# Attention and two MLP layers on one core: layer two takes its query tiles in pairs, with new PSUM shares and a new order

## The chip, the cores and the metric

One core of a Trainium2 chip runs the whole program. Its engines run side by side, each through its own list of instructions in order: TensorE (PE; its weight loads are shown as PEld), VectorE (DVE), ScalarE (ACT), GpSimd (POOL), and SyncE (SP), which here issues every DMA. They wait for each other by semaphores. The metric is the device time of one execution in microseconds (us); lower is better.

## The reference

Attention over 4 batches of 8 heads (576 queries and keys, head size 64), in which each query keeps its 32 largest scores; then two layers over the 2304 rows of 512 numbers. All in float32.

```python
scores = scale * np.matmul(q, k.transpose(0, 1, 3, 2))
kth = np.partition(scores, -top_k, axis=-1)[..., -top_k:-top_k + 1]
scores = np.where(scores >= kth, scores, -1000000000.0)
attn = np.exp(scores - np.max(scores, axis=-1, keepdims=True))
attn = attn / (np.sum(attn, axis=-1, keepdims=True) + 1e-09)
x = np.matmul(attn, v)                     # rows of 8 heads x 64 side by side
h = x @ w_in                               # layer 1: 512 -> 2048
x = np.maximum(0.01 * h, h) @ w_out        #          2048 -> 512
r = np.maximum(x @ w_in2, 0.0)             # layer 2
out = (s * (r * r) + b) @ w_out2
```

## The kernel before

**Precision.** Every float32 operand of a product is split into two float16 halves, a high and a low one, and a product is made of three: high by high, high by low, low by high. For that the rows and weights are first scaled by powers of two (`pow2_steps`).

**Query tiles and units.** The rows are 18 tiles of 128 queries; two of them are split and take 64 queries of each of two batches. A tile has four units of two heads, 72 in all. For a unit TensorE makes the scores (`qk`, L842; a split tile needs twice the products), ScalarE copies them out of PSUM (`s_ev`, L848), VectorE finds the 32 largest by four rounds of MAX8 (`t_max`, L860) and three of match-and-replace (`t_rep`, L869) per head, then exponentials and the mask follow either by way of VectorE (`expo`, `mask`, L882 and L885) or of POOL and ScalarE (`above`, `less`, `expo2`, L895 to L901); a letter of `MKE` and `MK` chooses for each unit. The result is cast to two halves (`e_hi` L970, `e_lo` L976) and turned by DMA (`e_turn`, L980); the first `EB` units are turned on TensorE instead (`e_tr2`, `e_sub`). TensorE multiplies by the values (`pv_mm`, L1010), VectorE brings the result out of PSUM (`x_ev`, L1017).

**Weights.** All four matrices are converted on the chip, each in 16 units of 128 columns or rows, four of them to a group with one scale: layer two's first (`2o`, `2i`), whose halves go back to DRAM (`sc16`), then layer one's (`1i`, `1o`), which stay in SBUF (`wreg`). A unit is loaded (`w_load`), rounded (`w_rest`, `w_shift`, `w_sign`, `w_round`), its group's norm is made on TensorE (`w_norm` L412, `sc_sum` L439), and it is split by one of five ways that a letter of `WM` names: `G` scales on VectorE (`pre`, L496) and `A` on ScalarE (L494), both with a subtraction on POOL (`lo_g`, L499); `D` uses ScalarE and VectorE (`lo_d`, L502); `P` and `V` multiply by a scaled identity on TensorE in float32 (`lo_t`, L507) into the ring `h`, copy the high half (`hi_p`, L513), and take the low half by another product and copy (`lo_s` L510, `lo_e` L516) or on VectorE (`lo_v`, L519). When all groups of layer one have their scales, `finals1` (the last line is L594) makes the constants without which no layer can start its activation.

**Layers.** `layer` makes one layer for one block of query tiles. `rows_in` scales, splits and turns the rows (a DMA, L1081). `m_in` (L1135) is 12 products that multiply one unit of the first weight, as stationary operand of 128 columns, by the block's turned rows; 512 columns fill a bank of the ring `h`. ScalarE and POOL make the two halves of the activation (`a1`, `a3`, `a4`, `a5`; L1164 to L1183). `m_out` (L1205) is 3 products for one unit of the second weight and one tile, 512 columns each, into the tile's bank `acc`. Layer one reads its weights from `wreg`. Layer two streams them from DRAM, two units (512 KB) a load (L1114), through four buffers (`wst`); one load of each weight is kept. `BLOCKS` has 16 blocks of one tile and one of two, for both layers; so layer two reads its weights 17 times.

**PSUM.** Eight banks: `tp` 2 (turned pieces, norms, sums, value products), `sc` 1 of two banks' size, `acc` 2, `h` 2.

**What sets the order.** The order of the instructions is not the engines' choice. `Plan` holds every step with an engine, an assumed duration, its dependences, the ring buffers it takes and a key. `order` plays the program once before it is built: whenever an engine is free it takes the ready step with the lowest key. The result is a fixed list per engine. The keys count in units of attention: `W0` and `WD` place the weights' conversion, `KO` the loads of keys, values and queries, and a layer's key `base` lies above all attention, so that layers fill TensorE between attention steps.

```python
        ready = {e: [] for e in set(self.eng)}
...
                heapq.heappush(ready[self.eng[n]], (self.key[n], n))
...
        base = 2.0 * sum(len(b) for b in blocks[:i]) + (1.0 if l else 0.0)
```

## Time and profile before

| | |
|---|---|
| median of 3 runs | 1210.54 us (1208.18 to 1210.85) |
| profiled execution, span | 1206.6 us |
| TensorE busy | 1044.3 us |
| VectorE, ScalarE, POOL busy | 918.5, 892.5, 844.5 us |
| DMA moved | 251.15 MB |

The page gives no other time for the profiled execution than its span, 3.9 us below the median of the runs. Idle time in one engine means little by itself; it matters on the engine that sets the end in that stretch. Records of products overlap in the trace, so the spacing of their starts is the price of a product, not the length of its record.

### The profile page before, as it was taken

The numbers are of one execution on the slowest core, as the hardware profiler recorded it, in microseconds if no ns is written. First come the engines' busy times: TensorE is split into PE (matmuls) and PEld (weight loads), VectorE is DVE, ScalarE is ACT, GpSimd is POOL, SyncE is SP. The second block draws the span as 40 slices with busy tenths as digits, with TensorE's granted clock in tenths as the row PEclk, the third lists the DMA queues.
The fourth block names the chain that finished last, engine by engine and source line by source line (L and its number), as shares of the span: only waits on it lengthen the run. The fifth ranks groups of instructions, "written<-read, shape, count | busy, mean of one in ns | idle before, by whom it ended". The sixth has DMA issues, their size and how long they took to land.

```text
span 1206.6 us, 30307 instructions
## 1 busy us (share of the span) xinstructions
PE 1044.3 (87%) x11589; PEld 754.8 (63%) x11589; DVE 918.5 (76%) x2164; ACT 892.5 (74%) x1696; POOL 844.5 (70%) x1169
## 2 busy tenths in 40 slices
PE   1675666239999999999999989999999999999988
...
GB/s 273 272 255 235 267 218 53 91 99 162 118 258 215 272 204 229 227 188 256 232 267 265 203 215 207 232 210 259 183 252 218 206 233 191 256 215 128 91 225 146
DMA packets 378289, 251.15 MB, mean 208 GB/s; under 512 B 281632, under 2 KB 306208, under 8 KB 378144
## 3 DMA queue, kind: packets, MB, share of 16 engines
...
q8 instruction: 90, 1.47, 0.5%
q14 instruction: 55, 0.45, 0.1%
...
## 4 chain that ended last, share of the span: by engine, by line
PE 43%; DVE 17%; DMA 12%; ACT 11%; POOL 11%; issue 4%; SPq 2%; DVEq 0%; POOLq 0%; ACTq 0%
PE h L1135 17%; PE acc L1205 17%; DVE mx L860 7%; DVE wk L869 6%; DMA st_o<-sc_2o 4%; PE pv L1010 3%; PE sc L842 3%; POOL ehl L976 2%; DMA a<-ehl 2%; POOL g L1183 2%; DMA st_i<-sc_2i 2%; POOL em L898 2%; ACT wreg L386 1%; ACT wreg L397 1%; ACT em L901 1%
## 5 line engine op out<-in xcount | busy, mean ns | idle before, releaser
L860 DVE MAX8 mx<-wk 128x8 f32<-128x576 f32 x432 | 313.2, 747 | 0.9
L1135 PEld LDWEIGHTS <-wreg 128*128 128x128 f16 x3264 | 211.0, 99 | 54.0 <-issue 6.4
L1135 PE MATMUL h<-early,wreg 128*128 128x128 f16 (+1 forms) x3264 | 235.1, 224 | 2.8 <-ACT r L1164 2.8
L1205 PE MATMUL acc<-wreg,g 128*128 128x512 f16 x864 | 231.3, 379 | 0.0
L1205 PEld LDWEIGHTS <-g 128*128 128x128 f16 x1728 | 154.8, 98 | 122.2 <-issue 17.3
L869 DVE MATCH_REPLACE8 wk<-mx,wk 128x576 f32<-128x576 f32 x288 | 212.8, 741 | 0.0
L1205 PE MATMUL acc<-st_o,g 128*128 128x512 f16 x756 | 200.6, 382 | 12.5 <-DMA st_o<-sc_2o 11.8
L1135 PEld LDWEIGHTS <-st_i 128*128 128x128 f16 x2856 | 179.7, 98 | 48.9 <-DMA st_i<-sc_2i 12.5
L1135 PE MATMUL h<-xT,st_i 128*128 128x128 f16 (+1 forms) x2856 | 201.4, 223 | 9.1 <-DMA st_i<-sc_2i 9.0
L976 POOL TENSOR_TENSOR ehl<-em,ehh 128x576 f16<-128x576 f32 x132 | 169.2, 1289 | 19.5 <-DMA a<-ehl 7.0
L898 POOL TENSOR_TENSOR em<-s,em 128x576 f32<-128x576 f32 x110 | 155.9, 1432 | 22.9 <-ACT em L895 22.7
L1183 POOL TENSOR_TENSOR g<-early,g 128x512 f16<-128x512 f32 x72 | 83.7, 1164 | 79.5 <-ACT g L1180 73.8
L842 PE MATMUL sc<-kT,qT 128*128 128x288 f16 (+1 forms) x640 | 102.3, 301 | 42.3 <-ACT s L848 36.4
L860 DVE MAX8 mx<-s 128x8 f32<-128x576 f32 x144 | 107.9, 750 | 23.0 <-ACT s L848 22.7
L1183 POOL TENSOR_TENSOR g<-r,g 128x512 f16<-128x512 f32 x72 | 84.4, 1172 | 49.7 <-ACT g L1180 49.3
L895 ACT ACTIVATE em<-s,st 128x576 f32<-128x576 f32 x110 | 82.2, 768 | 41.9 <-POOL st L889 37.5
L848 ACT COPY s<-sc 128x576 f32<-128x576 f32 x144 | 91.0, 632 | 23.5 <-PE sc L842 23.1
L901 ACT ACTIVATE em<-em,st,est 128x576 f32<-128x576 f32 x110 | 94.7, 862 | 17.1 <-POOL em L898 16.8
L869 DVE MATCH_REPLACE8 wk<-mx,s 128x576 f32<-128x576 f32 x144 | 106.8, 742 | 0.0
L1180 ACT ACTIVATE g<-r 128x512 f16<-128x512 f32 x144 | 89.5, 622 | 18.5 <-PE acc L1205 17.8
L842 PEld LDWEIGHTS <-qT 128*128 128x128 f16 (+1 forms) x640 | 56.9, 105 | 70.7 <-issue 49.9
L1167 ACT ACTIVATE r<-h,cg 128x512 f32<-128x512 f32 x72 | 49.1, 682 | 67.0 <-PE h L1135 65.9
...
## 6 DMA issues: line engine op xcount, KB each, us to landing
st_i<-sc_2i SPq DMA_DIRECT2D x119, 512.0 KB, 4.9
st_o<-sc_2o SPq DMA_DIRECT2D x119, 512.0 KB, 5.1
wreg<-in_moe_w_in_dram SPq DMA_DIRECT2D x32, 512.0 KB, 5.2
wreg<-in_moe_w_out_dram SPq DMA_DIRECT2D x16, 512.0 KB, 5.0
raw_1o<-in_moe_w_out_dram SPq DMA_DIRECT2D x16, 512.0 KB, 4.2
...
```

The lines of the kernel that those rows point to most:

```text
L842: nc.tensor.matmul(pt[a, c, 0:288], lhsT=qT[u][:, h, z, a], rhs=kT[b, p][:, 576 * h + 288 * c:576 * h + 288 * c + 288], start=(z == 0), st ...
L848: nc.scalar.copy(sc[u, h], box["pt"][:, :, 0:288])
L860: nc.vector.max(out=mx[u][:, h, r, :], in_=wk[u, h] if r else flat(sc[u, h]))
L869: nc.vector.match_replace(out=wk[u, h], in_to_replace=mx[u][:, h, r, :], in_values=src, imm_value=NEG)
L895: nc.scalar.activation(em[u][:, h, :], flat(sc[u, h]), AF.Relu, bias=st[u][:, 8 + h:9 + h], scale=-BIG)
L898: nc.gpsimd.tensor_tensor(em[u][:, h, :], flat(sc[u, h]), em[u][:, h, :], op=ALU.subtract)
L901: nc.scalar.activation(em[u][:, h, :], em[u][:, h, :], AF.Exp, bias=st[u][:, h:h + 1], scale=est[:, 0, u:u + 1], accum_out=st[u][:, 2 + h: ...
L976: nc.gpsimd.tensor_tensor(ehl[u][1][:, a], em[u][:, h, :], ehl[u][0][:, a], op=ALU.subtract)
L1135: nc.tensor.matmul(box["h"][:, n * T:(n + 1) * T], lhsT=w[:, ew, c, :], rhs=src[:, ex, c, :], start=(c == 0 and ew == 0 and ex == 0), stop ...
L1180: nc.scalar.activation(gt[:, 0], box["r1"], AF.Square if l else AF.Copy)
L1183: nc.gpsimd.tensor_tensor(ghl[i, l, g][:, 1], box["v"], ghl[i, l, g][:, 0], op=ALU.subtract)
L1205: nc.tensor.matmul(accs[i, l, tt], lhsT=ghl[i, l, g][:, eg, n * T + tt * P:n * T + (tt + 1) * P], rhs=w[:, ew], start=(f == 0 and eg == 0 ...
```

## The change

Five things change together.

- `BLOCKS` becomes nine pairs and holds for layer two alone; layer one takes each tile by itself. Layer two's `m_in` has 256 columns (two weight units fill a bank of `h`), and one loaded weight serves two tiles. The two tiles' rows for layer two (`xT1`) are one buffer; each tile's rows for layer one (`xT0`) get their own, four of half the size.
- PSUM: `tp` goes from two banks to one, `acc` from two to three. The norms (`w_norm`) and the column sums (`csum`) move from `tp` to `acc`.
- The letters: `WM` sends all 16 units of `1i` through TensorE (`P`), `2o` by `V` and `P`, `2i` by `P` and `A`, `1o` by `A` and `D`; `MK` and `MKE` have four masks fewer on VectorE; `EB` is 4 instead of 6.
- The finishing instructions `f1`, `f3`, `f4` use one-tensor forms with a scalar per row.
- The order: all keys are new, and ten tables add an offset to each step's key (of a unit's attention, of a weight's rounding, halves and load, of keys, values, queries, layers and rows). Some assumed durations are new too.

```diff
-        "ahh": 1, "ahl": 1, "x32": 1, "xs": 2, "xhl": 3, "xT0": 2, "xT1": 2, "r1": 2, "r2": 2, "g": 3, "raw": 2, "T": 8, "hl": 8, "wraw": 4, "wT": 8, "wst": 4,
-        "tp": 2, "sc": 1, "acc": 2, "h": 2, "lane": 1, "fin": 4, "nred": 1, "cI": 1}
-WM = {"1i": "PDAA", "1o": "DAAG", "2o": "GPPV", "2i": "PPAV"}
+        "ahh": 1, "ahl": 1, "x32": 1, "xs": 2, "xhl": 3, "xT0": 4, "xT1": 2, "r1": 2, "r2": 2, "g": 3, "raw": 2, "T": 8, "hl": 8, "wraw": 4, "wT": 8, "wst": 4,
+        "tp": 1, "sc": 1, "acc": 3, "h": 2, "lane": 1, "fin": 4, "nred": 1, "cI": 1}
+WM = {"1i": "PPPP", "1o": "ADAA", "2o": "VPVV", "2i": "PAPP"}
-MK = "DAAAAA"
-MKE = "DADADADAAAAADADAAADADADA"
+MK = "AAAADA"
+MKE = "DADAAADADAAAAAAADAAADADA"
-EB = 6
+EB = 4
-W0 = {"2o": -38.54, "2i": -51.71, "1i": -9.33, "1o": 3.35}
+W0 = {"2o": -44.539, "2i": -30.313, "1i": -18.009, "1o": 31.234}
-BLOCKS = [1, 1, 1, 1, 1, 1, 1, 1, 1, 1, 1, 1, 1, 1, 1, 1, 2]
+BLOCKS = [2, 2, 2, 2, 2, 2, 2, 2, 2]
+L2AT = 15.899
...
-        kk = wkey[m, f] - 100.0
+        oi = order.index((m, f))
+        kk = wkey[m, f] - 100.0 + WX[oi]
...
-            gram[m, gi] = ring("tp", [P, 512], F32, f"gram_{m}_{gi}")
+            gram[m, gi] = ring("acc", [P, 512], F32, f"gram_{m}_{gi}")
...
-                x = add(PE, 0.86, lo_t, [i_], ks, take=[th] + out_tok, use=tI + [tT])
+                x = add(PE, 1.05, lo_t, [i_], ks, take=[th] + out_tok, use=tI + [tT])
...
-    blocks, t = [], 0
+    blocks, t = ([[t] for t in range(NTL)], []), 0
     for n in BLOCKS:
-        blocks.append(list(range(t, t + n)))
+        blocks[1].append(list(range(t, t + n)))
         t += n
...
-        base = 2.0 * sum(len(b) for b in blocks[:i]) + (1.0 if l else 0.0)
+        base = 2.0 * blocks[l][i][-1] + (L2AT + PX[i] if l else TX[i])
...
-    for i, bl in enumerate(blocks):
-        tX = token("xT0")
-        ready = []
-        for n, t in enumerate(bl):
-            ready.append(rows_in(i, n, 0, lambda t=t: x32[t], x_done[t], [tok_x[t]], tX, 4.0 * t + 3.5 - 100.0))
-        tY[i] = token("xT1")
-        acc = layer(i, 0, tX, ready, tY[i])
-        y_ready[i] = []
-        for n, t in enumerate(bl):
-            y_ready[i].append(rows_in(i, n, 1, lambda i=i, n=n: accs[i, 0, n], [done[i, 0, n]], [acc[n]], tY[i], -150.0))
-        acc = layer(i, 1, tY[i], y_ready[i], None)
-        for n, t in enumerate(bl):
+    for i, pair in enumerate(blocks[1]):
+        tY, y_ready = token("xT1"), []
+        for n, t in enumerate(pair):
+            tX = token("xT0")
+            ready = rows_in(t, 0, 0, lambda t=t: x32[t], x_done[t], [tok_x[t]], tX, 4.0 * t + 3.5 - 100.0 + RX[t])
+            acc = layer(t, 0, tX, [ready], None if n else tY)
+            y_ready.append(rows_in(i, n, 1, lambda t=t: accs[t, 0, 0], [done[t, 0, 0]], [acc[0]], tY, -150.0))
+        acc = layer(i, 1, tY, y_ready, None)
+        for n, t in enumerate(pair):
...
-                nc.vector.tensor_tensor(f[:, 0:1], pw[:, 0, t:t + 1], pw[:, 1, t:t + 1], op=ALU.mult)
+                nc.vector.tensor_scalar(f[:, 0:1], pw[:, 0, t:t + 1], pw[:, 1, t:t + 1], None, op0=ALU.mult)
```

**TensorE at the first accumulation.** The names hold unit and head (`sc_11_0` is unit 11, head 0), weight and group (`gram_1o_3`), and block, layer and tile (`acc_0_0_0`). Before:

```order
L842 MATMUL sc_10_1_2338<-kT2_107,qT_10_1547 128x288
...
L412 MATMUL gram_1o_3_2350<-T_1o_12_2223 128x128
...
L439 MATMUL gram_1o_3_2350<-nrm_89,ones_74 128x1
...
L842 MATMUL sc_11_0_2406<-kT3_111,qT_10_1547 128x288
...
L507 MATMUL wlo_1i_12_2461<-wreg_64,cI_1i_3_1972 128x512
...
L1135 MATMUL h_0_0_1_2468<-early_63,wreg_64 128x128
...
L510 MATMUL wlo_1i_12_2461<-wreg_64,negI16_72 128x512
...
L1205 MATMUL acc_0_0_0_2531<-wreg_64,g_0_0_0_2464 128x512
```

The last norm of layer one's weights (`gram_1o_3`) stands ahead of unit 11's scores, and the first product into `acc` in that unit. Now:

```order
L856 MATMUL sc_11_1_2461<-kT3_111,qT_10_1589 128x288
...
L425 MATMUL gram_1o_3_2536<-T_1o_12_2402 128x128
...
L1024 MATMUL pv_9_2561<-vhl1_100,a0_9_2492 128x128
...
L452 MATMUL gram_1o_3_2536<-nrm_89,ones_74 128x1
...
L856 MATMUL sc_12_0_2593<-kT0_99,qT_12_1806 128x288
...
L856 MATMUL sc_12_1_2607<-kT0_99,qT_12_1806 128x288
...
L1149 MATMUL h_0_0_2_2666<-early_63,wreg_64 128x128
...
L1149 MATMUL h_0_0_3_2728<-early_63,wreg_64 128x128
...
L1219 MATMUL acc_0_0_0_2744<-wreg_64,g_0_0_0_2680 128x512
```

The last norm stands a unit later, ahead of unit 12's scores, and both of that unit's heads come ahead of the first accumulation; ten units' value products stand before it instead of nine.

**TensorE in layer two.** `h_15_1_2` is block 15, layer two, third bank of `h`; `st_15_i_4` the streamed weight. Before, late in the program:

```order
L1135 MATMUL h_15_1_2_18302<-xT1_15_17832,st_15_i_4_17974 128x128
...
L1205 MATMUL acc_16_0_0_17892<-wreg_64,g_16_0_7_18232 128x512
...
L1135 MATMUL h_15_1_2_18302<-xT1_15_17832,st_15_i_5_18186 128x128
...
L1135 MATMUL h_15_1_3_18371<-xT1_15_17832,st_15_i_6_18298 128x128
...
L1205 MATMUL acc_15_1_0_18430<-kept_o_0_2665,g_15_1_0_18200 128x512
...
L1205 MATMUL acc_15_1_0_18430<-st_15_o_1_18266,g_15_1_0_18200 128x512
```

A streamed `w_in` load serves 24 products of 128 columns, a `w_out` load 6 products, and one tile is accumulated at a time. Now, for the pair 7:

```order
L1149 MATMUL h_7_1_4_16729<-xT1_7_15114,st_7_i_4_16621 128x256
...
L1219 MATMUL acc_7_1_1_16635<-st_7_o_1_16184,g_7_1_1_16633 128x512
...
L1149 MATMUL h_7_1_4_16729<-xT1_7_15114,st_7_i_4_16621 128x256
...
L1219 MATMUL acc_7_1_0_16625<-st_7_o_2_16682,g_7_1_2_16700 128x512
...
L1149 MATMUL h_7_1_5_16771<-xT1_7_15114,st_7_i_5_16725 128x256
...
L1219 MATMUL acc_7_1_1_16635<-st_7_o_2_16682,g_7_1_2_16700 128x512
```

The same load serves 24 products of 256 columns, and the two tiles' accumulators take turns with one `w_out` weight.

**SP's queue.** `st_9_i_5` is a load of layer two's `w_in` for block 9; the others are transposes and loads for attention. Before:

```order
L1114 DMA st_9_i_5_12656<-sc16_2i_94 128x2x1024
L812 DMA_TRANSPOSE qT_58_12679<-qhl_58_12304 128x8x128
L980 DMA_TRANSPOSE a0_51_12702<-ehh_51_12618 128x9x128
L980 DMA_TRANSPOSE a1_51_12727<-ehl_51_12639 128x9x128
L1114 DMA st_9_o_1_12761<-sc16_2o_95 128x2x1024
L1114 DMA st_9_i_6_12771<-sc16_2i_94 128x2x1024
L676 DMA_TRANSPOSE kT4_115<-khl_3_2_12559 128x9x128
L1114 DMA st_9_i_7_12861<-sc16_2i_94 128x2x1024
L1114 DMA st_9_o_2_12895<-sc16_2o_95 128x2x1024
L1114 DMA st_9_o_3_12915<-sc16_2o_95 128x2x1024
```

Now, for the pair 4:

```order
L1128 DMA st_4_i_5_12229<-sc16_2i_94 128x2x1024
L1128 DMA st_4_o_3_12233<-sc16_2o_95 128x2x1024
L1128 DMA st_4_i_6_12239<-sc16_2i_94 128x2x1024
L1128 DMA st_4_o_4_12285<-sc16_2o_95 128x2x1024
L994 DMA_TRANSPOSE a0_54_12313<-ehh_54_12287 128x9x128
L994 DMA_TRANSPOSE a1_54_12338<-ehl_54_12290 128x9x128
L1128 DMA st_4_i_7_12357<-sc16_2i_94 128x2x1024
L639 DMA vn_3_3_12379<-in_v_dram 128x2x256
L642 DMA vn_3_3_12379<-in_v_dram 64x64 x2
L1128 DMA st_4_o_5_12445<-sc16_2o_95 128x2x1024
```

Loads of the two weights alternate, and there are 126 of them in the program instead of 238.

## Rows read from the trace of the kernel before

**Rows 1.** The page: busy us, share of the span and instructions of each engine.

```profile
PE 1044.3 (87%) x11589; PEld 754.8 (63%) x11589; DVE 918.5 (76%) x2164; ACT 892.5 (74%) x1696; POOL 844.5 (70%) x1169
```

**Rows 2.** Busy us (instructions) by stretch; then granted clock, DMA share, GB/s.

```profile
0.00:180.00 180.00, 104.22 (x551) 61.23 (x552) 138.68 (x307) 151.30 (x297) 132.54 (x166) 0.79 0.86 255
180.00:271.00 91.00, 38.48 (x325) 28.25 (x324) 81.61 (x178) 69.81 (x131) 71.23 (x85) 0.62 0.34 81
277.50:345.00 67.50, 65.85 (x837) 49.90 (x836) 65.54 (x164) 51.22 (x97) 48.43 (x67) 1.00 0.89 177
345.00:1054.00 709.00, 688.51 (x8625) 513.89 (x8623) 617.91 (x1472) 560.29 (x1071) 547.62 (x811) 1.00 0.97 227
1054.00:1202.00 148.00, 141.27 (x1209) 96.38 (x1208) 6.94 (x28) 54.58 (x92) 40.81 (x38) 0.99 0.54 164
```

**Rows 3.** Timeline around the first accumulation: start us, us, engine, line, operation.

```profile
271.26 0.15 DVE L594 SCALAR_TENSOR_TENSOR cg<-cg 128x4 f32<-128x4 f32 x1
...
277.68 0.81 PE L1205 MATMUL acc<-wreg,g 128*128 128x512 f16 x3
```

**Rows 4.** Waits of TensorE from 277.5 us: total us, times, longest.

```profile
PE acc L1205 <- DMA st_o<-sc_2o: 11.8, 12, 2.5
PE h L1135 <- DMA st_i<-sc_2i: 9.0, 9, 4.1
```

**Rows 5.** Timeline of TensorE in two stretches; starts give the spacing.

```profile
858.54 1.94 PE L1010 MATMUL pv<-vhl,a 128*64 128x128 f16 x54
860.42 0.84 PE L1135 MATMUL h<-xT,kept_i 128*128 128x128 f16 x12
...
866.69 0.65 PE L842 MATMUL sc<-kT,qT 128*128 128x288 f16 x4
867.18 0.83 PE L1135 MATMUL h<-xT,st_i 128*128 128x128 f16 x12
867.85 0.81 PE L1205 MATMUL acc<-kept_o,g 128*128 128x512 f16 x3
868.49 0.83 PE L1135 MATMUL h<-xT,st_i 128*128 128x128 f16 x12
...
1174.54 1.47 PE L1135 MATMUL h<-xT,st_i 128*128 128x256 f16 x12
1175.85 0.81 PE L1205 MATMUL acc<-st_o,g 128*128 128x512 f16 x3
```

**Rows 6.** Groups by line: count, busy us and mean ns of one, idle before.

```profile
L860 DVE MAX8 mx<-wk 128x8 f32<-128x576 f32 x432 | 313.2, 747 | 0.9
...
L976 POOL TENSOR_TENSOR ehl<-em,ehh 128x576 f16<-128x576 f32 x132 | 169.2, 1289 | 19.5 <-DMA a<-ehl 7.0 <-ACT ehh L970 6.4 <-ACT khl L648 3.7
...
L901 ACT ACTIVATE em<-em,st,est 128x576 f32<-128x576 f32 x110 | 94.7, 862 | 17.1 <-POOL em L898 16.8
...
L970 ACT CAST ehh<-em 128x576 f16<-128x576 f32 x132 | 88.0, 667 | 4.4 <-DVE em L885 3.8
...
L496 DVE TENSOR_SCALAR T_1o<-T_1o,cg 128x512 f32<-128x512 f32 x4 | 3.3, 832 | 0.0
...
L513 ACT CAST wreg<-wlo_2o 128x512 f16<-128x512 f32 x12 | 6.9, 579 | 3.8 <-PE wlo_2o L507 3.8
```

**Rows 7.** The fp32 products of one weight: duration ns min/median/max, first and last start.

```profile
L507 PE MATMUL wlo_1i<-wreg,cI_1i x8: 592/1061/1221, 159.9 to 268.4; 128*128 128x512 f32 x8
```

**Rows 8.** Groups by line: weight load, value evacuation, finishing instruction.

```profile
L1135 PEld LDWEIGHTS <-st_i 128*128 128x128 f16 x2856 | 179.7, 98 | 48.9 <-DMA st_i<-sc_2i 12.5 <-issue 1.1
...
L1017 DVE TENSOR_TENSOR x<-pv,st 128x128 f32<-128x128 f32 x72 | 20.3, 282 | 22.9 <-PE pv L1010 22.8
...
L1250 DVE TENSOR_TENSOR fin<-pw 128x1 f32<-128x1 f32 x18 | 8.5, 473 | 0.0
```

**Rows 9.** The page, DMA issues: count, KB each, us to landing.

```profile
st_i<-sc_2i SPq DMA_DIRECT2D x119, 512.0 KB, 4.9
```

80 lines of the change are left out of this document (45 added, 35 removed).

## The prediction

> **What bounds the kernel now.** I read the busy line of the page first: TensorE is busy for 1044.3 of 1206.6 us, the most of any engine [rows 1]. That is an average over two different stages, so the table by stretches comes next [rows 2]. Up to 271 us TensorE is busy for 104.2 + 38.5 = 142.7 us; VectorE is busy for 138.7 + 81.6 = 220.3 us, and for 90% of the stretch from 180 to 271 us. From 277.5 us on TensorE is busy for 65.9 of 67.5, 688.5 of 709 and 141.3 of 148 us, at full clock, while VectorE has slack up to 1054 us and is nearly done after it. So two stages: until about 271 us the conversion of weights and the first attention units, carried by VectorE and ScalarE; after it a stream of TensorE work that no other engine holds up for long.
>
> The seam is sharp. The first product of a layer's second weight needs `finals1`, the scales over all of layer one's weights. In the timeline `finals1` ends at 271.26 us and the first product into an accumulator starts at 277.68 us [rows 3]. I call this start the gate. Behind it TensorE idles for 1.65 + 20.49 + 6.73 = 28.9 us, and the view of waits says on what: 11.8 us for streamed `st_o` weights and 9.0 us for `st_i`, 20.8 us in all; the rest is spread thin [rows 4].
>
> So the time is the gate, plus TensorE's work behind it, plus 28.9 us, plus the end. By the order, behind the gate stand 504 dozens of 128-column products (0.67 us each), 32 dozens of 256 columns (1.31 us), 576 triples of 512 columns (0.64 us), 105 score groups and 16 double ones (0.49 us, double 0.98), and value products of 55 units and 8 double ones (0.94 and 1.88 us) [rows 5]: 337.7 + 41.9 + 368.6 + 67.1 + 66.7 = 882 us. 277.7 + 882 + 28.9 = 1188.6; the 18 us that are missing to 1206.6 are the last output after the last product and a per cent or two by which these prices are low. I carry them over unchanged. What decides is therefore how the change moves three terms: the gate, the work behind it, the idle time in it.
>
> **Term one, the work behind the gate.** The order behind the first accumulation has 6048 products of 128 columns and 384 of 256 columns before, 3300 and 1728 now; 1728 products of 512 columns in both. Twelve products of 128 columns take 867.85 - 867.18 = 0.67 us, twelve of 256 columns 1175.85 - 1174.54 = 1.31 us [rows 5]. That is 56 and 109 ns each: the narrow product already runs at nearly the rate per column of the wide one. Taken away are 229 dozens at 0.67 = 153.4 us, added 112 dozens at 1.31 = 146.7 us: -6.7 us. Three score groups move ahead of the gate (867.18 - 866.69 = 0.49 us each, 1.5 us), and one unit's value products (half of the 860.42 - 858.54 = 1.88 us of a double unit, 0.9 us) [rows 5]. Sum: -9 us. Bounds: the starts are given to 0.01 us, which is 3.4 us over 229 + 112 dozens; -6 to -12.
>
> The Trainium skill says otherwise (TensorE: Matmul & The Clock Gate, section Back-to-back issue gap): with a weight load before each product, 128 columns are said to sustain about 81 ns. By that figure the 229 dozens would cost 223 us and this term would be -78 us, an estimate; the trace's 56 ns contradicts it.
>
> **Term two, the gate.** Up to `finals1` the new order puts more on VectorE: 15 more MAX8 and 10 more replacements (1.9 units of attention more), 4 more subtractions from PSUM, but 5 fewer `lo_d` and 7 fewer `pre` (both gone from this engine by the new letters in WM). At 0.747 us for the first three kinds and 0.832 for the others [rows 6]: 29 x 0.747 - 12 x 0.832 = 21.7 - 10.0 = +11.7 us. ScalarE: 30 more copies out of `h`, 21 fewer casts and scalings, 12 fewer copies of transposes, all at about 0.58 us; 8 more casts of `em`, 4 more score copies and 2 more `above` at 0.667, 4 more exponentials at 0.862 [rows 6]: 30, 21 and 12 give -1.7, the others +12.8, together +11 us. POOL: 8 more `ehl` (1.289 us) and 2 more masks against 12 fewer `lo_g` of the same size: about 0 [rows 6]. VectorE is 90% busy there, so 11.7 / 0.90 = 13 us: gate at 291.
>
> TensorE gets 16 more fp32 products for weights (44 instead of 28). One takes two records of about 1.06 us each in `wlo_1i` (8 records for 4 products) [rows 7]; 16 x 2 = 32 us, and 12 more subtractions, against 18 fewer transposes and 6 fewer of their subtractions. I take this at nothing, for TensorE is idle for 271 - 142.7 = 128 us there; uncovered it is the slower rival below. The clock is granted at 0.62 in 180 to 271 us [rows 2], a mix of the 1.2 and 2.4 GHz levels, and more products there can raise it; that cannot cost. Bounds of the gate: 277 us (POOL's term decides), 307 us (half of the 32 us on top of VectorE's 13).
>
> **Term three, the idle time.** Streamed loads fall from 238 to 126, of 512 KB each. A load lands 4.9 us after its issue [rows 9], and four buffers hold two weight units each. Before, a buffer of `w_in` serves two dozens of 128 columns, 1.34 us; where layer two runs alone four buffers last 5.4 us, hardly more than one landing. Now it serves two dozens of 256 columns, 2.62 us, and a buffer of `w_out` four triples instead of two; four buffers last 10.5 us. The new order also alternates the two kinds (`i`, `o`, `i`, `o`) at most three of one kind in a row, where before up to six followed each other. I keep 5 of the 20.8 us: -16 us. Bounds: 0, if the waits stay as they are, and -20.8.
>
> **Edits at nothing.** The pair makes layer two wait for both tiles' rows; between the last product of tile 17's layer one and the first of the last pair's layer two stand 12 dozens and 18 triples of another pair (27 us), which cover its row's casts and transpose, and the last block was a pair before too. The finishing arithmetic (18 times three VectorE instructions, the first at 473 ns [rows 8]) loses its two-tensor forms; VectorE isn't the bound behind the gate, and after 1054 us it has 6.9 us of work in 148 [rows 2]. The four masks that leave VectorE, and the two units whose transposes move to the DMA queue, lie beside TensorE's stream as well; e_turn transposes share SP's queue with the loads, of which 112 are gone.
>
> One bank for `tp` instead of two: the evacuation of a unit's values takes 0.282 us on VectorE [rows 8], and the next user of the bank stands some 10 us of layer products later on TensorE. I cost it at nothing. A rule of the Trainium skill speaks against this edit (Perfetto Trace Analysis, section Matmuls): independent groups of products should rotate through different PSUM banks, so that evacuating one overlaps the next. No row here shows a wait for that bank; by the rule each of the 72 evacuations would be exposed.
>
> **Sum.** 1206.6 + 13 - 9 - 16 = 1194.6 us for the profiled execution. The median of the runs shown is 1210.5, 3.9 us above that execution; with the same distance the forecast is 1198 us, its own range 1188 to 1208.
>
> **Rivals.**
> - The waits come back under another name. The queue of SP runs in order, and a load behind a transpose that waits for POOL starts late however few loads there are; pairs take their weights in denser bursts. Against it: twice the time per buffer. If all 20.8 us stay: 1198 + 16 = 1214, within 1207 to 1218.
> - Slower: the weights' conversion goes through TensorE and the two `h` banks. A fp32 product, a copy, a subtracting product and a second copy follow each other, and the unit holds its bank throughout; all of layer one's 16 first weights take this way now, 4 before. It decides from the point where TensorE's 32 us are not hidden behind VectorE's 13: up to 32 - 13 = 19 us later, 1198 + 20 = 1218. For it: these products run with records of about 1.06 us, twice the 0.49 us that a score group of four products takes, at a clock that is granted at 0.62 [rows 2, 7]. Against it: TensorE's 128 idle us there.
> - Faster: the gate does not move, because VectorE's extra units fill its idle 19% of the first 271 us: 1198 - 13 = 1185.
> - The one bank shows: 72 x 0.282 = 20 us, 1218.
> - Weight loads pace the narrow products: a load has a record of 98 ns [rows 8]; if that were the spacing, 229 dozens would give up 2748 x 42 ns = 115 us more, 1083. The 56 ns in the timeline exclude it, short of a fault in the records.
>
> **How the numbers follow.** Forecast 0.48, waits that stay 0.18, gate that stays 0.17, conversion through TensorE 0.13, the bank 0.03, weight loads 0.01. The likeliest gives 1198 us. A measurement of this kernel tells about 0.2% from no change, that is 2.4 us: faster is below 1208.1, slower above 1213. Faster: 0.45 of the forecast's 0.48, 0.17, 0.02 of the waits' case and 0.01: 0.65. Same: 0.02 and 0.09: 0.11. Slower: 0.01 + 0.07 + 0.13 + 0.03 = 0.24. The range 1183 to 1217 leaves out the far half of the case in which the gate moves little or even forward (0.06) and most of the two cases at 1218 (0.12).
>
> **What would show it.** Gate: the first product into `acc` at about 291 us; at 278 the third rival is right, past 300 the second. Work: dozens at 1.31 us in layer two, and from gate to last product about 12 + 876 us. Idle: TensorE's waits for `st_i` and `st_o` together near 5 us. The forecast is wrong if TensorE idles more than 30 us behind the gate, above all on products that wait for `acc`, `tp` or a row's transpose, or if VectorE or ScalarE become the releaser there.

## The result and the profile after

The changed kernel takes 1163.99 us (median of 4 runs, 1161.46 to 1166.86) against 1209.74 us, also of 4 runs (the 1210.54 above is of the first three): a ratio of 0.963, 95% interval 0.9605 to 0.9657. The direction was forecast, the size was not: 45.7 us less where the forecast was 12.5 less, and below the stated range of 1183 to 1217. The profiled execution has a span of 1159.7 us, 46.9 us less than that of before.

The page's busy line answers to [rows 1]: TensorE's share rises from 87 to 89%.

```profile
PE 1034.9 (89%) x10265; PEld 725.4 (63%) x10265; DVE 899.7 (78%) x2148; ACT 894.5 (77%) x1704; POOL 839.9 (72%) x1167
```

The gate first: the end of `finals1` (now L607) and the first product into `acc` (now L1219) in the timeline, columns as in [rows 3].

```profile
259.79 0.15 DVE L607 SCALAR_TENSOR_TENSOR cg<-cg 128x4 f32<-128x4 f32 x1
...
265.97 0.81 PE L1219 MATMUL acc<-wreg,g 128*128 128x512 f16 x3
```

Against [rows 3] `finals1` starts its last instruction 11.5 us earlier and the first product into `acc` starts 11.7 us earlier, where I had put it 13 us later. The table by stretches, columns as in [rows 2]: the first 180 us, on to `finals1`, the beginning of the stream, attention, layer two alone. The last row of the five is followed by one for the whole stream.

```profile
0.00:180.00 180.00, 108.72 (x587) 58.61 (x588) 148.54 (x348) 163.47 (x324) 133.71 (x169) 0.88 0.87 255
180.00:259.00 79.00, 42.05 (x398) 28.12 (x396) 75.96 (x171) 67.88 (x128) 69.06 (x97) 0.69 0.57 126
265.70:333.00 67.30, 64.47 (x790) 46.36 (x788) 64.86 (x161) 52.20 (x102) 55.59 (x80) 1.00 0.68 135
333.00:1010.00 677.00, 669.56 (x7207) 487.83 (x7205) 594.22 (x1428) 551.81 (x1054) 533.78 (x780) 1.00 0.74 159
1010.00:1155.70 145.70, 144.99 (x1239) 99.48 (x1236) 8.50 (x27) 54.71 (x92) 43.20 (x41) 1.00 0.47 140
...
265.70:1155.70 890.00, 879.02 (x9230) 633.67 (x9227) 667.58 (x1614) 658.72 (x1246) 632.57 (x900) 1.00 0.69 154
```

From the gate to the last product TensorE idles for 890.0 - 879.0 = 11.0 us, 28.9 before. Its waits for streamed weights in that stretch (total us, times, longest), against 9.0 for `st_i` and 11.8 for `st_o` in [rows 4]:

```profile
PE h L1149 <- DMA st_i<-sc_2i: 1.5, 2, 1.1
...
PE acc L1219 <- DMA st_o<-sc_2o: 0.6, 1, 0.6
```

So the three terms of the forecast's sum, forecast and measured: gate +13 and -11.7; work behind it -9 and 879.0 - 896.2 = -17.2; idle time in it -16 and -17.9. Measured, -46.8; the end after the last product is unchanged (3.9 and 3.8 us).

### The profile page after: what moved, and what is told of

It reads as the page before. It is cut to its first block, busy times and chain, and to the rows that moved or that the text cites. A ratio compares the mean times of both kernels' runs of the same rounds, so it can differ in the third digit from the quotient of the medians.

```text
span 1159.7 us, 27441 instructions
## 1 busy us (share of the span) xinstructions
PE 1034.9 (89%) x10265; PEld 725.4 (63%) x10265; DVE 899.7 (78%) x2148; ACT 894.5 (77%) x1704; POOL 839.9 (72%) x1167
## 3 DMA queue, kind: packets, MB, share of 16 engines
q8 instruction: 80, 1.31, 0.5%
## 4 chain that ended last, share of the span: by engine, by line
PE 60%; ACT 15%; DMA 8%; DVE 8%; POOL 5%; issue 3%; SPq 1%; DVEq 0%; ACTq 0%; POOLq 0%
PE h L1149 25%; PE acc L1219 24%; PE pv L1024 4%; PE sc L856 4%; DVE mx L874 3%; DMA a<-ehl 2%; DVE wk L883 2%; ACT em L915 2%; ACT wreg L399 2%; ACT wreg L410 2%; ACT s L862 1%; POOL ehl L990 1%; POOL g L1197 1%; DMA qT<-qhl 1%; POOL em L912 1%
## 5 line engine op out<-in xcount | busy, mean ns | idle before, releaser
L1149 PEld LDWEIGHTS <-wreg 128*128 128x128 f16 x3456 | 214.6, 98 | 60.2 <-issue 11.5
L1149 PE MATMUL h<-early,wreg 128*128 128x128 f16 x3456 | 236.0, 220 | 9.8 <-ACT r L1178 8.1
L1219 PEld LDWEIGHTS <-g 128*128 128x128 f16 x1728 | 157.7, 98 | 113.9 <-issue 3.1
L1219 PE MATMUL acc<-wreg,g 128*128 128x512 f16 x864 | 226.4, 379 | 0.2 <-POOL g L1197 0.2
L1219 PE MATMUL acc<-st_o,g 128*128 128x512 f16 x756 | 195.9, 379 | 1.3 <-ACT g L1194 0.7
L1149 PE MATMUL h<-xT,st_i 128*128 128x256 f16 x1512 | 185.0, 273 | 1.6 <-DMA st_i<-sc_2i 1.5
L990 POOL TENSOR_TENSOR ehl<-em,ehh 128x576 f16<-128x576 f32 x136 | 176.1, 1298 | 12.1 <-ACT ehh L984 10.0
L1149 PEld LDWEIGHTS <-st_i 128*128 128x128 f16 x1512 | 147.5, 98 | 44.8 <-DMA st_i<-sc_2i 3.1
L912 POOL TENSOR_TENSOR em<-s,em 128x576 f32<-128x576 f32 x114 | 162.3, 1439 | 16.3 <-ACT em L909 16.1
L874 DVE MAX8 mx<-s 128x8 f32<-128x576 f32 x144 | 108.1, 750 | 20.8 <-ACT s L862 20.6
L915 ACT ACTIVATE em<-em,st,est 128x576 f32<-128x576 f32 x114 | 98.6, 865 | 18.4 <-POOL em L912 18.2
L862 ACT COPY s<-sc 128x576 f32<-128x576 f32 x144 | 91.2, 634 | 17.5 <-PE sc L856 17.2
L1181 ACT ACTIVATE r<-h,cg 128x512 f32<-128x512 f32 x72 | 49.2, 683 | 64.6 <-PE h L1149 64.2
L1178 ACT ACTIVATE r<-h,cg 128x512 f32<-128x512 f32 x72 | 49.0, 682 | 60.2 <-PE h L1149 52.9
```

Of the source, the lines that this page charges most:

```text
L862: nc.scalar.copy(sc[u, h], box["pt"][:, :, 0:288])
L874: nc.vector.max(out=mx[u][:, h, r, :], in_=wk[u, h] if r else flat(sc[u, h]))
L912: nc.gpsimd.tensor_tensor(em[u][:, h, :], flat(sc[u, h]), em[u][:, h, :], op=ALU.subtract)
L915: nc.scalar.activation(em[u][:, h, :], em[u][:, h, :], AF.Exp, bias=st[u][:, h:h + 1], scale=est[:, 0, u:u + 1], accum_out=st[u][:, 2 + h: ...
L990: nc.gpsimd.tensor_tensor(ehl[u][1][:, a], em[u][:, h, :], ehl[u][0][:, a], op=ALU.subtract)
L1149: nc.tensor.matmul(box["h"][:, n * T:(n + 1) * T], lhsT=w[:, ew, c, :], rhs=src[:, ex, c, :], start=(c == 0 and ew == 0 and ex == 0), stop ...
```

## The experiments

The table shows what each kernel's profiled execution has in these terms (us; the gate is the start of the first product into `acc`, work and idle are TensorE's busy and other time from there to its last product). "17th unit" is when VectorE starts that unit's first MAX8, the 129th in the program: how far attention has come. "Use" is VectorE's busy share up to the end of `finals1`. Times are counted from the first busy instruction, 0.2 us later than in the views. In the kernels a_conv0, a_psum, a_wst2, a_kvq0 and a_w0_10 a dependence keeps the second tile of a pair behind the first.

| kernel | median | ratio to before, 95% | gate | work | idle | 17th unit | use |
|---|---|---|---|---|---|---|---|
| before | 1209.7 | | 277.4 | 896.1 | 28.9 | 340 | 0.81 |
| b_letters | 1216.5 | 1.006 [1.0033, 1.0089] | 262.7 | 900.6 | 41.3 | 335 | 0.80 |
| b_psumlet | 1208.6 | 0.998 [0.9956, 0.9995] | 248.2 | 903.5 | 48.3 | 325 | 0.80 |
| a_single | 1199.9 | 0.991 [0.9889, 0.9934] | 267.1 | 890.1 | 36.5 | 309 | 0.86 |
| a_lay0 | 1174.5 | 0.970 [0.9676, 0.9729] | 265.4 | 882.0 | 21.5 | 307 | 0.87 |
| changed | 1164.0 | 0.963 [0.9605, 0.9657] | 265.7 | 878.9 | 11.0 | 308 | 0.87 |
| b_w0_12 | 1235.7 | 1.020 [1.0169, 1.0232] | 256.2 | 907.1 | 69.3 | 355 | 0.80 |
| b_fin | 1208.4 | 0.999 [0.9968, 1.0017] | 271.8 | 895.9 | 34.8 | 338 | 0.82 |
| b_delay2 | 1231.7 | 1.017 [1.0135, 1.0206] | 296.7 | 896.5 | 37.8 | 360 | |
| b_pairs | 1258.4 | 1.038 [1.0335, 1.0416] | 277.1 | 901.9 | 71.5 | 345 | 0.84 |
| a_conv0 | 1248.8 | 1.032 [1.029, 1.0342] | 350.8 | 870.8 | 20.3 | 308 | 0.86 |
| a_psum | 1193.3 | 0.986 [0.9824, 0.9901] | 279.6 | 884.6 | 20.3 | 310 | 0.85 |
| a_wm | 1193.8 | 0.987 [0.9835, 0.9897] | 307.2 | 874.1 | 11.9 | 320 | 0.83 |
| a_kvq0 | 1194.2 | 0.986 [0.982, 0.99] | 299.1 | 873.3 | 14.3 | 311 | 0.84 |
| a_w0_10 | 1194.4 | 0.986 [0.9826, 0.9901] | 268.9 | 890.6 | 32.7 | 327 | 0.83 |
| a_wst2 | 1255.0 | 1.035 [1.0281, 1.0411] | 263.0 | 899.0 | 75.5 | 305 | 0.88 |
| a_delay | 1186.4 | 0.979 [0.9756, 0.9829] | 286.1 | 879.8 | 14.7 | 328 | |
| a_delay2 | 1189.7 | 0.982 [0.9788, 0.9856] | 267.5 | 884.4 | 31.2 | 332 | |
| a_fin | 1163.7 | 0.961 [0.9586, 0.9634] | 261.3 | 881.6 | 16.4 | 308 | 0.85 |

The first six rows are a ladder from the kernel before to the changed one.

**b_letters: the letters alone.**

```diff
-WM = {"1i": "PDAA", "1o": "DAAG", "2o": "GPPV", "2i": "PPAV"}
+WM = {"1i": "PPPP", "1o": "ADAA", "2o": "VPVV", "2i": "PAPP"}
...
+EB = 4
```

> The kernel before with the letters of the changed kernel alone (WM, MK, MKE, EB): 16 more fp32 products on TensorE for 1i, fewer lo_d and pre on VectorE. Theory A: finals1 stands behind 238 instead of 246 us of VectorE's work in the order; gate about 9 us earlier, 268; time about 1201. Rival (the way through TensorE and the two h banks is the slow one): gate at 290 or later, TensorE's waits for copies out of h above 20 us up to the gate, time 1218 or more. Rival (letters change nothing, VectorE's load is not what sets the gate): gate 277, 1210.

The gate came 15 us earlier, and the time did not fall; it rose by 0.3 to 0.9%. The profiled execution, at a span of 1208.9, is below the median, and its terms are those of the table. From the gate to the last product:

```profile
262.70:1204.50 941.80, 900.47 (x10638) 661.80 (x10635) 696.16 (x1661) 672.03 (x1270) 648.18 (x926) 0.99 0.87 210
```

Idle 941.8 - 900.5 = 41.3 us: what the gate gave, 14.7 us, came back as 12.4 us of idle time and 4.5 of work. The 17th unit was only 5 us earlier. The conversion through TensorE did not delay the gate, against the slower rival of the forecast.

**b_psumlet: letters and PSUM shares.**

```diff
-        "tp": 2, "sc": 1, "acc": 2, "h": 2, "lane": 1, "fin": 4, "nred": 1, "cI": 1}
+        "tp": 1, "sc": 1, "acc": 3, "h": 2, "lane": 1, "fin": 4, "nred": 1, "cI": 1}
...
+            gram[m, gi] = ring("acc", [P, 512], F32, f"gram_{m}_{gi}")
```

> The kernel before with the letters and the PSUM shares of the changed kernel (tp 1, acc 3, norms and column sums in acc), without pairs and without new keys. In the order finals1 stands after 8.6 units (219 us of VectorE's work) instead of 10.4 (246). Theory A: finals1 at about 241 us, gate about 248, 1.75 units of TensorE's attention behind it (3 us): time about 1184. Rival (one bank for tp shows): waits of TensorE for tp or for evacuations of pv above 10 us behind the gate, time 1195 to 1215. Rival (VectorE's work only put off): gate 248, idle behind it up by 25 us, about 1208.

The gate came as theory A had it (248.2), the time did not: idle rose by 19 us, work by 7. The rival in which VectorE's work is only put off had the time (1208) and nearly the idle time (25 us). No wait for `tp` stands among TensorE's larger waits.

**b_w0_12: finals1 first by a key.**

```diff
-W0 = {"2o": -38.54, "2i": -51.71, "1i": -9.33, "1o": 3.35}
+W0 = {"2o": -38.54, "2i": -51.71, "1i": -9.33, "1o": -8.65}
```

> The kernel before with one number changed: the keys of the conversion of 1o lie 12 units earlier (W0 3.35 -> -8.65). In the order finals1 now stands after 7.5 units of attention on VectorE instead of 10.4. Theory A (the gate sets the time, and the order sets the gate): VectorE's work ahead of finals1 falls by 32 us of 246, at the use of before finals1 comes at about 236 us and the first product into acc at about 242 instead of 277.5; three units of scores and values, 1.9 us each, go behind it; time about 1210 - 35 + 6 = 1181 us. Rival B (VectorE's work is only put off: behind the gate it becomes the bound, or TensorE finds no attention to fill with): gate at 242, but TensorE's idle time behind it grows by about 30 us, time 1205 to 1212. Rival C (the conversion of weights is a chain of its own that cannot go faster): gate stays at 270 or later, time 1205 to 1215.

All theories missed the time: the gate came 21 us earlier and the time was 2% longer. Rival B had the kind of loss, idle time behind the gate, but not its size. Attention was pushed back (17th unit +15 us), idle behind the gate rose by 40 us, work by 11.

**b_pairs: pairs in both layers.**

```diff
-BLOCKS = [1, 1, 1, 1, 1, 1, 1, 1, 1, 1, 1, 1, 1, 1, 1, 1, 2]
+BLOCKS = [2] * 9
```

> The kernel before with BLOCKS of nine pairs, for both layers, nothing else. Products behind the gate: 3024 of 256 columns fewer-for-6048 of 128 at 56.7 ns: 343 us become 331 us at 109.4 ns, -12 us; streamed loads 126 instead of 238. In the order finals1 moves 4 us of VectorE's work later. Theory A: waits for st_i and st_o fall from 20.8 to about 4 us, -17; gate +4: time about 1210 - 12 - 17 + 4 = 1185. Rival (the waits for streamed weights stay): 1202. Rival (a pair waits for both tiles, TensorE starves near the gate and at the end): idle behind the gate above 40 us, time 1215 or more.

The rival that TensorE starves held, though not only near the gate and at the end. The waits for streamed weights did fall (7.4 + 3.0 us behind the gate), but the score products waited for ScalarE to copy the scores before them out of PSUM:

```profile
PE sc L842 <- ACT s L848: 36.2, 19, 6.0
...
PE acc L1205 <- DMA st_o<-sc_2o: 7.4, 4, 4.1
...
PE h L1135 <- DMA st_i<-sc_2i: 3.0, 2, 2.1
```

Three stretches of 75 us (columns as in [rows 2]) show a second loss: in two of them TensorE is busy for 61 to 62 us and the granted clock is 0.89, a mix of its two levels, so that the busy time itself holds slower products; in the third it is busy for 73.7 us at 1.00.

```profile
425.00:500.00 75.00, 61.35 (x532) 41.84 (x531) 73.35 (x173) 55.73 (x107) 54.11 (x85) 0.89 0.61 122
575.00:650.00 75.00, 61.77 (x527) 44.40 (x527) 64.31 (x156) 65.35 (x130) 59.22 (x99) 0.89 0.76 180
650.00:725.00 75.00, 73.65 (x654) 51.20 (x653) 72.29 (x173) 59.80 (x115) 63.31 (x94) 1.00 0.59 117
```

So work rose by 6 us instead of falling by 12. The changed kernel keeps layer one single; whether that is what makes its pairs pay isn't shown, for no run pairs layer two alone in the kernel before.

**a_conv0: conversion's offsets zero.**

```diff
+WX = [0.0] * 64
+HX = [0.0] * 64
+LX = [0.0] * 64
```

> The changed kernel with the three offset tables of the weights' conversion (of rounding, halves and load) set to zero; a dependence keeps the second tile of a pair behind the first (it moves no instruction of the changed kernel itself). In the order finals1 stands after 19 units of attention instead of 12.25, behind 342 us of VectorE's work instead of 259. Theory A (the gate sets the time, the order sets the gate): finals1 near 340 us, gate near 347, 81 us later than 265.7; 6.75 units of attention, 1.9 us each, move ahead of it: time about 1164 + 81 - 13 = 1232. Rival (TensorE catches up, since other engines have run ahead with attention and the layers behind the gate run without holes): 1164 to 1185.

The gate went 85 us later with attention on time (17th unit at 308), and the time rose by 85 us. A gate that is last does set the time.

**a_lay0: offsets of layers and rows zero.**

```diff
+TX = [0.0] * 18
+PX = [0.0] * 9
+RX = [0.0] * 18
```

> The changed kernel with the offsets of the layers' and rows' keys (three tables) set to zero. Up to the gate the order is the same. Theory A: gate 265.7 unchanged; the tables only smooth the order of TensorE's stream, idle time behind the gate grows from 11 to 15 us: time about 1168. Rival (the tables of the layers make the idle time small, not the pairs): idle behind the gate near 30 us, waits for st_i and st_o above 10 us, 1183.

Idle is 21.5 instead of 11.0 us, work 3 us more; the median rose by 10.5 us, to between the two cases (1168 and 1183). Waits for the streams stay small (2.5 and 1.8 us); the tables smooth other waits, mostly of the value products for their turned attention (6.0 us instead of 2.1) and for POOL's halves of the activation (3.9 instead of 0.2).

**a_single: layer two one tile at a time.**

```diff
-BLOCKS = [2, 2, 2, 2, 2, 2, 2, 2, 2]
+BLOCKS = [1] * 16 + [2]
-L2AT = 15.899
+L2AT = 1.0
```

(`TX` and `PX` are zero, as in a_lay0; `RX` is not.)

> The changed kernel with layer two in blocks of one tile (16 of one, the last of two), the layers' offsets zero and layer two's key right behind layer one's (offset 1.0). Up to the gate the order is the same as in the changed kernel. 238 streamed loads instead of 126, 128-column products in layer two. Theory A (pairs give the work and the idle time, not the gate): gate 265.7 unchanged, products of m_in +10 us, waits for st_i and st_o back at 15 to 21 us: time about 1164 + 10 + 18 = 1192. Rival (the waits went by the new order, not by the loads): waits for the streams below 5 us, time about 1175.

Against a_lay0 the kernel is 25.5 us slower: work +8.1, idle +15.0, gate +1.7. The waits behind the gate are those of before:

```profile
PE h L1149 <- DMA st_i<-sc_2i: 14.6, 14, 3.0
...
PE acc L1219 <- DMA st_o<-sc_2o: 6.8, 11, 1.5
```

This is the forecast's price of the pairs, -6.7 and -16 us, nearly to the number. Mixed in are layer two's key and `RX`, which differ too. With this the ladder is complete: letters and PSUM shares together -2 us, the new keys (with the buffers of `xT0` and the finishing forms) -9, pairs -25, the layers' tables -10. These are prices in this order of steps only: taken back from the changed kernel by itself, the PSUM shares' edit is worth 29 us (a_psum) and that of `WM` 30 (a_wm). In those runs the tables stay as they are for the changed kernel's order, so a part of such a price can be that they no longer fit.

**a_psum: the PSUM shares of before in the changed kernel.**

```diff
-        "tp": 1, "sc": 1, "acc": 3, "h": 2, "lane": 1, "fin": 4, "nred": 1, "cI": 1}
+        "tp": 2, "sc": 1, "acc": 2, "h": 2, "lane": 1, "fin": 4, "nred": 1, "cI": 1}
```

> The changed kernel with the PSUM shares of before (tp 2, acc 2; norms and column sums still in acc). In the order finals1 stands after 13.4 units instead of 12.25, behind 274 us of VectorE's work instead of 259. Theory A: finals1 near 274, gate near 280, 14 us later, 2 us of attention ahead; and with two accumulators a pair leaves no bank for the next layer one, so TensorE's waits for acc grow by 5 to 20 us: time 1181 to 1196. Rival (PSUM shares don't matter): 1164. Rival (one tp bank costs): faster than 1164, waits for pv's evacuation gone.

The time, 1193.3, is within the expected range: gate +14, idle +9, work +6. The reason is so for the gate alone. The expected waits for a free accumulator don't show (0.7 us); behind the gate TensorE waits for `st_o` (7.3 us) and for turned attention (4.4).

**a_wst2: two stream buffers instead of four.**

```diff
-"wst": 4
+"wst": 2
```

> The changed kernel with two buffers for streamed weights instead of four; up to the gate the order is the same. Theory A (the waits fell because a buffer lasts twice as long): two buffers last as long as four did before where layer two runs alone, 5.2 us against a landing of 4.5 us; waits of TensorE for st_i and st_o return, 15 to 30 us instead of 2: time about 1180 to 1195. Rival (the new order places the loads so well that buffers don't matter): waits below 6 us, 1164 to 1170.

The waits returned, and with more than was expected:

```profile
PE acc L1222 <- DMA st_o<-sc_2o: 28.3, 34, 3.0
PE h L1151 <- DMA st_i<-sc_2i: 21.4, 25, 2.6
```

So it is the time that the buffers last, not a placing of the loads, that removed them. The time, 1255, is far past the 1180 to 1195 expected. Besides the 49.7 us of these waits, TensorE waited 16.2 us for turned attention, and its work rose by 20 us (a product of 256 columns took 113.1 ns instead of 109.5); why was not tried.

**a_delay: 90 VectorE instructions in finals1.**

```diff
+        for _ in range(90):
+            nc.vector.tensor_scalar(pad, pad, 1.0, None, op0=ALU.mult)
         nc.vector.scalar_tensor_tensor(cg[:, 0, 3, :], ...
```

> The changed kernel with 90 short VectorE instructions (64 columns each, on a scratch tile that nothing uses) put into finals1, ahead of its last instruction; the order is the same. Estimated from rows of the trace at 0.13 us each, 12 us. Theory A (the gate is a term of the sum, one for one): first product into acc at 278 instead of 265.7, idle behind it unchanged near 11 us: time about 1176. Rival B (an earlier or later gate is made good behind it, as in the kernel before with its letters alone, whose gate came 15 us earlier and whose time did not fall): idle behind the gate falls by half or more, time 1164 to 1170.

In VectorE's timeline the padding is the row here:

```profile
258.89 20.59 DVE L610 TENSOR_SCALAR pad<-pad 128x64 f32<-128x64 f32 x90
```

It took 20.6 us, not 12, and the gate moved by 20.4, the time by 22.4. I read that as one for one, theory A. It had moved two things, though: the gate and all that stood behind on VectorE.

**a_w0_10: finals1 first by a key, in the changed kernel.**

```diff
-W0 = {"2o": -44.539, "2i": -30.313, "1i": -18.009, "1o": 31.234}
+W0 = {"2o": -44.539, "2i": -30.313, "1i": -18.009, "1o": 21.234}
```

> The changed kernel with the keys of the conversion of 1o 10 units earlier (31.2 -> 21.2); a dependence keeps the second tile of a pair behind the first, which alone moves nothing. In the order finals1 stands after 11.4 units instead of 12.25, behind 250 us of VectorE's work instead of 259. Theory A: gate 9 us earlier at 257, one unit of attention behind it (+2): time about 1157. Rival B (an earlier gate with less attention ahead of it leaves TensorE short of work, as the three kernels before with earlier gates: 41 to 69 us idle behind it): idle behind the gate 20 us or more, time 1164 to 1175.

Theory A missed even the gate: it came 3 us later, with less attention ahead of it, for VectorE's use fell to 0.83. Rival B had the idle time (32.7 us) and not the time. The 17th unit was 19 us later and the time 30 us longer.

**a_kvq0: offsets of attention and its loads zero.**

```diff
+UX = [0.0] * 72
+KX = [0.0] * 16
+VX = [0.0] * 16
+QX = [0.0] * 18
```

> The changed kernel with the offsets of the units' attention and of the loads of keys, values and queries (four tables) set to zero, conversion and layers as they are. In the order finals1 stands after 14.4 units, behind 285 us of VectorE's work instead of 259. If VectorE's use ahead of finals1 stays at the changed kernel's 0.87: finals1 near 286, gate near 292, two units of attention ahead of it (-4): time about 1187. If these tables are what raised the use from 0.81: finals1 at 305 or later, time 1205 or more. Rival (gate made good behind it): 1164 to 1175.

Use fell to 0.84: gate +33, time +30, between the two cases (1187 and 1205).

**a_fin and b_fin: an earlier gate at the same order.** After the order is made, `finals1` moves up to behind the last scale, and the first activations ahead of four conversions on ScalarE:

```diff
     steps = plan.order()
+    last = max(steps.index(d) for d in plan.deps[fin1])
+    steps.remove(fin1)
+    steps.insert(last + 1, fin1)
...
+    steps[at:at] = early_acts
```

> The changed kernel with two moves in its finished order and no other: finals1 goes ahead of the nine VectorE instructions (5.3 us) that stand between the last scale of 1o and it, and the first four activation steps of layer one on ScalarE go ahead of the four conversions (2.3 us) that stand before them. The same attention stands ahead of the gate on TensorE. Theory A (one for one, as with the delay): first activation at about 254.6 instead of 259.97, gate 5 us earlier at 260.5, time about 1159. Rival B (an earlier gate is given back as idle behind it): gate 260.5, idle behind it 15 us or more, 1163 to 1165. Rival C (VectorE's attention, put off by 4.4 us, comes back as a wait of TensorE for scores or values): time 1164 to 1168.

> The kernel before with the same two moves: finals1 ahead of seven VectorE instructions (4.9 us), the first activation of layer one ahead of four ScalarE conversions. Theory A: first activation at about 266.5 instead of 271.45, gate at 272.5 to 273, time 5 us shorter, about 1205. Rival B (given back as idle, as with the letters): gate 273, idle behind it 33 us or more, time 1209 to 1211. Rival C (another step holds the first accumulation, as the low half of 1i that stands between TensorE's first products): gate moves by 2 us or less, 1208 to 1210.

Rival B in both (b_fin's median lies 0.6 us below that rival's range). The gates came 4.4 and 5.6 us earlier, the times are the same as without (0.961 beside 0.963, and 0.999). Idle behind the gate rose by 5.4 and 5.9 us. In a_fin TensorE's timeline shows where more than half of it went, two products after the new gate:

```profile
261.57 0.59 PE L1219 MATMUL acc<-wreg,g 128*128 128x512 f16 x2
265.17 0.39 PE L1219 MATMUL acc<-wreg,g 128*128 128x512 f16 x1 [3.00 <-POOL g L1197]
```

The third product waited 3.0 us for POOL, whose queue had not been moved.

**a_wm: the letters of before in the changed kernel.**

```diff
+WM = {"1i": "PDAA", "1o": "DAAG", "2o": "GPPV", "2i": "PPAV"}
```

> The changed kernel with the letters WM of before (four units of 1i instead of 16 by way of TensorE); everything else, the tables too, as changed. In the order finals1 stands after 14.4 units, behind 292 us of VectorE's work instead of 259. If the new keys raise VectorE's use by themselves: use 0.86 to 0.87 again, finals1 near 293, gate near 299, 4 us of attention ahead of it, time about 1194. If the letters were what raised it: use 0.81, finals1 near 313, gate near 319, time about 1213. Rival (the conversion through TensorE costs time, so the old letters are the better ones here too): below 1164.

The time, 1193.8, is the one expected for the keys, but the mechanism is not: use 0.83 and a gate at 307 lie between the two cases. It does not tell letters from keys: the changed kernel's order does worse with each part that was taken back.

**a_delay2 and b_delay2: the same instructions behind finals1.**

```diff
         nc.vector.scalar_tensor_tensor(cg[:, 0, 3, :], ...
+        for _ in range(90):
+            nc.vector.tensor_scalar(pad, pad, 1.0, None, op0=ALU.mult)
```

> The changed kernel with the same 90 VectorE instructions as the delay run (20.6 us there), now put behind the last instruction of finals1 instead of ahead of it: layer one's activation and the gate stay where they are, and only VectorE's attention behind it is 20.6 us later. Theory A (the gate sets the time): gate 265.7, time within 5 us of 1164, since TensorE has layer products to fill with. Theory D (two fronts: TensorE's order mixes layers and attention, so attention that comes later holds the stream as much as a later gate does): idle behind the gate up by 15 to 20 us, 17th unit at 328 instead of 308, time 1180 to 1187, as in the delay run.

> The kernel before with the same 90 VectorE instructions (about 20.6 us) behind the last instruction of its finals1; gate unchanged at 277.5. Theory D: VectorE's attention is the front that is last in this kernel (its gate 5.6 us earlier gave nothing): time up by 18 to 22 us, about 1230. Theory A: within 5 us of 1210. Rival (VectorE has slack behind the gate in this kernel and makes good a part): up by 8 to 12, about 1220.

The times are near theory D's in both: +25.7 us with the gate 1.8 us later (1189.7, a little past its 1187), and +20.0 in the kernel before (by the medians of that comparison, 1231.74 and 1211.74). The delay was not the same, though: the padding took 20.59 us in b_delay2, as in a_delay, but 25.65 in a_delay2, in VectorE's timeline:

```profile
261.02 25.65 DVE L611 TENSOR_SCALAR pad<-pad 128x64 f32<-128x64 f32 x90
```

There five of the 90 began while a POOL instruction ran; they took 1.08 to 1.33 us and ended 50 ns after it, where the others took 0.195. So in both runs the time rose by what VectorE lost, one for one. What TensorE waited for first was not attention. In a_delay2 it is the low half of one of layer one's weights, made on VectorE behind the padding, in TensorE's timeline:

```profile
295.90 1.01 PE L1223 MATMUL acc<-wreg,g 128*128 128x512 f16 x2 [15.38 <-DVE wreg L515]
```

In b_delay2 one wait of 19.4 us, for a copy of a weight out of `h` whose engine had waited for VectorE, held the gate itself, 19.3 us later; theory D had that gate unchanged, so this run is one more delayed gate and no test of it. So the runs show that VectorE's queue, whatever stands in it, sets the time around the gate; they do not separate attention in it from the last weights.

## Why the forecast was wrong

**The step that failed: "VectorE is 90% busy there, so 11.7 / 0.90 = 13 us: gate at 291".** The gate came 11.7 us earlier instead of 13 later. Of the 34.8 us between the forecast's -12 and the measured -46.8, 24.7 are booked in the gate, 8.2 in the work behind it and 1.9 in the idle time. A gate that moves forward had a part of 0.06 in the forecast's chances. Two faults are in the step that failed, and a third lies behind it.

The work was over-counted a little. VectorE's busy time up to `finals1` rose from 220.7 to 225.4 us, +4.7. Counted by kind it was +18 for attention, -10 for `pre` and `lo_d`, +2 for `lo_v`, as forecast; but instructions that the change left alone ran shorter. These rows by line up to `finals1`, of before and then of after, show the roundings (48 of them) and a four-times repeated step of one column:

```profile
L391 DVE SCALAR_TENSOR_TENSOR wreg<-wreg 128x512 int32<-128x512 int32 x48 | 47.3, 1003 | 15.8 <-ACT wreg L386 15.7
...
L568 DVE SCALAR_TENSOR_TENSOR cg<-cg,sb 128x1 f32<-128x1 f32 x4 | 3.2, 804 | 0.0
```

```profile
L404 DVE SCALAR_TENSOR_TENSOR wreg<-wreg 128x512 int32<-128x512 int32 x48 | 44.4, 929 | 8.3 <-ACT wreg L399 8.3
...
L581 DVE SCALAR_TENSOR_TENSOR cg<-cg,sb 128x1 f32<-128x1 f32 x4 | 0.6, 144 | 0.0
```

Both follow what POOL does at that moment. Before, each of the four one-column steps began during a POOL instruction and ended 14 to 22 ns after it; after the change none did. One of each in the timelines of POOL and VectorE:

```profile
62.66 1.48 POOL L401 TENSOR_TENSOR wreg<-wreg 128x512 int32<-128x512 int32 x1
63.64 0.52 DVE L568 SCALAR_TENSOR_TENSOR cg<-cg,sb 128x1 f32<-128x1 f32 x1
```

```profile
62.21 0.14 DVE L581 SCALAR_TENSOR_TENSOR cg<-cg,sb 128x1 f32<-128x1 f32 x1
62.45 1.30 POOL L414 TENSOR_TENSOR wreg<-wreg 128x512 int32<-128x512 int32 x1 [0.78 <-DVE cg L581]
```

Of these 48 roundings, those that began with POOL idle took 0.66 to 0.69 us in either kernel (17 before, 15 after). The others took 1.18 us on average before and 1.04 after, and most of them ended 0.55 us after POOL's instruction. So a part of VectorE's busy time is waiting for POOL, and it changes with the order too.

The larger fault is the constant use. The share 0.90 was that of one stretch, 180 to 271 us; over the whole of the first stage it was 220.7 / 271.2 = 0.81, and the new order has 225.4 / 259.7 = 0.87. VectorE's idle time ahead of `finals1` fell from 50.5 to 34.3 us, by 16; the rows by line above show half of it, the roundings' wait for ScalarE, 15.7 to 8.3 us. The rival that VectorE's extra units fill its idle time went the right way and not far enough. Use was 0.80 in both kernels with the old keys and the new letters (b_letters, b_psumlet), 0.84 in b_pairs with neither, 0.86 in a_single with letters, PSUM shares and new keys together, 0.83 to 0.85 where the changed kernel lost its letters, its PSUM shares or the attention's tables. Which of them alone would do is not settled: the new keys without the letters and shares were not tried.

The third fault: the gate was taken for a term that pays by itself. The sum of the three terms holds as bookkeeping in every run, but its terms are not free of each other. A gate that is last costs one for one (a_conv0). A gate that is made earlier gives nothing by itself (b_fin, a_fin, and b_letters, where the letters move with it): TensorE's list mixes layer products with attention's and waits there for other engines instead. [rows 2] had the sign of it: from 277.5 to 345 us VectorE was busy for 65.5 of 67.5 us, and I wrote that it had slack up to 1054. What the change did was to bring forward both: the gate by 12 us and attention by 32 us at the 17th unit. a_single has both early too (267 and 309) and no pairs; with its gate 10.3 us earlier, its profiled execution is 8.9 us shorter than that of before. That the earlier attention is what lets the gate's gain stand is argued from these runs; none moves attention alone.

**The work behind the gate: right in kind, 8 us short.** The spacings of after are those of before; in the timeline twelve products of 128 columns take 1051.12 - 1050.45 = 0.67 us and twelve of 256 take 1102.77 - 1101.46 = 1.31 us:

```profile
1050.45 0.83 PE L1149 MATMUL h<-early,wreg 128*128 128x128 f16 x12
1051.12 0.81 PE L1219 MATMUL acc<-wreg,g 128*128 128x512 f16 x3
...
1101.46 1.47 PE L1149 MATMUL h<-xT,st_i 128*128 128x256 f16 x12
1102.77 0.81 PE L1219 MATMUL acc<-st_o,g 128*128 128x512 f16 x3
```

Over the whole stream (start to next start, idle left out) a 128-column product takes 56.7 ns before and 56.1 after, one of 256 columns 109.4 and 109.5: 384.7 us of them before, 374.2 after, -10.5 instead of -6.7, a little past the 3.4 us that the two decimals of a start left open. The value products are 3.1 us less instead of 0.9, the 1728 `m_out` products 1.7 us less where I had nothing; the score products are 1.3 less, where I had 1.5.

The Trainium skill's 81 ns for a sustained 128-column product with its weight load (TensorE: Matmul & The Clock Gate, section Back-to-back issue gap) is not what these runs show: 56 ns, at full granted clock, in both kernels.

**The idle time: right, in part by luck.** -17.9 for -16. The reason held: with pairs undone the waits for the streams are back at 21.4 us (a_single), with half of the buffers at 49.7 (a_wst2), and the pairs are worth 15.0 us of idle time. But two terms that I did not have nearly cancel: idle time rose by 7.6 us from the kernel before to a_single, with the earlier gate, and the layers' tables took off 10.5 (a_lay0).

**Edits at nothing.** The single `tp` bank shows no wait behind the gate: of TensorE's 11.0 us of idle time there, the view of waits puts 10.3 down to ScalarE, POOL and DMA and none to VectorE, which empties that bank of values. The finishing step's first instruction fell from 473 [rows 8] to a mean of 201 ns, in the shade of TensorE: in the old form the 8 that began with POOL idle took 0.15 us and the other 10 took 0.73, each ending within 22 ns of POOL's instruction; the new form takes 0.2 us either way. The fp32 products of `1i` cost TensorE less than the two records of 1.06 us that [rows 7] gave: all 16 of them, 32 records, take 20.6 us, where I had 32. Shortest and longest are as before, but the median is lower, at a granted clock that in the first 180 us rose from 0.79 [rows 2] to 0.88 (min, median, max in ns):

```profile
L520 PE MATMUL wlo_1i<-wreg,cI_1i x32: 592/686/1222, 141.3 to 201.4; 128*128 128x512 f32 x32
```

The rival of waits that stay is excluded by the waits for streamed weights above (2.1 us), the slower one through TensorE and `h` by b_letters and by the gate itself.
